# Attention numerators: high and low part of the left operand in one pass

## The chip, the cores and the metric

One core of a Trainium2 chip runs the whole program. The metric is the device time of one execution in microseconds; lower is better. A core has TensorE (PE: matmuls, with its weight loads shown as PEld), VectorE (DVE), ScalarE (ACT), GpSimd (POOL) and SyncE (SP), which issues all the transfers here.

## The reference

The input x has 2048 rows of 1024 columns. It is normalized, goes through a linear attention with 32 heads of 32 columns and through a gated unit, and both are joined:

```
xn = layernorm(x)
q, k, v = split_heads(xn @ wqkv)
phi(a) = concat(softmax(a @ w_phi), softmax(-(a @ w_phi)))   # 64 features a head
kv  = sum over rows of phi(k)^T v          # per head 64 x 32
num = phi(q) @ kv
den = phi(q) . (sum over rows of phi(k)) + 1e-6
s = (num / den) @ wo
g = silu((sigmoid(xn @ w_gate) * (xn @ w_up)) @ w_down)
out = x + s * g
```

All inputs and the output are float32.

## The kernel before

Large products take operands of the type F32R, each float32 operand cut in two parts, with three products in place of one. `split` (L122 to L125) writes a high part with a ScalarE cast (L124) and the rest with a VectorE subtraction (L125). `mm3` (L127 to L131) then adds high x high, high x low and low x high in a bank of PSUM; these are lines 129, 130 and 131 of the profile. The products over blocks use seven block products in place of eight (names B11, T2, T3, B21, T1, T4, B22), which is why there are so many sums of blocks.

The stages follow one another: normalization and the folding of the weights; the projections for the first half of the rows and their gated products; the same for the second half; the down products; the result products. A deque of background tasks is worked off beside the matmuls, one task after certain evacuations. The order of the instructions on each engine is not only that of the source: the program is built with a planner that simulates a timeline (`schedule_with_timeline_sim=True`) and orders what is ready by its own costs. What it writes down for an engine is then fixed.

**Block building.** For each half `hb` of the heads (16 heads), `k_task` and `kv_products` sum phi(k) and v products over all rows. `kv_sum` gathers them, and `kv_blocks` (L471) turns them into left operands: a chunk is 128 rows of features (two heads) and 128 columns, and only the 64 columns of its own two heads are filled. Chunks go in twos, b = 0 and 1: chunk b fills columns 64b to 64b+63, and the other 64 are set to zero. High and low part lie in two planes of a slot. Four chunks make one slot, so a half has two slots; four stores to `kvbd_d` (L489) keep them, and at step n = 20 of the down products four loads (L935) bring them into the slots of `KVB`.

**The attention stage.** There are 8 pairs of row tiles (256 rows). For a pair, `attend` (L672) lists 12 tasks, six for each half of the heads: four `phi_transpose` and two `numerator`, q = 0 and 1 (a quarter of the heads). `phi_transpose` (L625) turns a tile of phi(q), already divided by its denominator, with four transposes (L630) into a bank of the ring `tpr` and splits it. `numerator` (L639) multiplies the four chunks of its quarter with it: chunks 2j and 2j+1 add into the same 256 columns of one bank of the ring `nmr`, which has two banks, so the zeros of one leave the rows of the other alone. A ScalarE copy (L648) takes the whole bank to `oraw[hb]`. After q = 1, `o_operands` (L655) makes the seven blocks from the two halves: splits on ScalarE and VectorE, differences on GpSimd (L660, L663, L664, L668).

The tasks of pair 0 run beside the end of the down products. Those of pair `tp_ + 1` are spread over the 28 `mm3` of the result products of pair `tp_`, whose accumulations use the ring `amm` of four banks. There, B11 is copied to a result buffer by ScalarE (L1008), T2, T3 and the others are added by VectorE (L1010, L1012, L1019, L1022), multiplied and added by GpSimd (L1023, L1024) and stored (L1025). Four result buffers serve a pair and are used again by the next, so the copy at L1008 waits for a store of the pair before.

Of the kernel before, what the change touches and what calls it, by code (L numbers as in the profile page):

```python
# [9 lines left out]
F32 = mybir.dt.float32  # L10
# [7 lines left out]
P = 128  # L18
# [8 lines left out]
HB = 512  # L27
# [21 lines left out]
def hedgehog_glu_kernel(  # L49
# [11 lines left out]
    nc = tc.nc  # L61
# [4 lines left out]
    dram = ctx.enter_context(tc.tile_pool(name="dram", bufs=1, space=DRAM))  # L66
# [8 lines left out]
    e_d = dram.tile([TT, 2, P, 2 * HB], F32, name="e_d")  # L75
    r_d = dram.tile([CTT, 2, P, 32], F32, name="r_d")
    zb_d = dram.tile([2, P, 2 * HB], F32, name="zb_d")
    kvbd_d = dram.tile([4, P, 2, HB], F32, name="kvbd_d")
    ws_d = dram.tile([2 * NJ, 4, P, 2 * HB], F32, name="ws_d")
    h_d = dram.tile([7, NJ, P, NCH, HB], F32, name="h_d")  # L80
    wd_d = dram.tile([7, NJ, P, HB], F32, name="wd_d")
# [3 lines left out]
    slots, blocks, where = {}, {}, {}  # L85

    def block(name, first, n, dtype):
        again = blocks.get(name, (None, 0))[1]
        t = sb.tile([P, n, 2, HB], dtype, name=f"{name}_{again}", tag=name, bufs=1)
        blocks[name] = t, again + 1  # L90
        for i in range(n):
            slots[first + i] = t[:, i]
            where[first + i] = name, i
        return t
# [13 lines left out]
    def whole(i):  # L108
        return slots[i].rearrange("p a n -> p (a n)")
# [9 lines left out]
    def pair(i):  # L119
        return slots[i][:, 0], slots[i][:, 1]  # L120

    def split(o, src):  # L122

        nc.scalar.copy(o[0], src)  # L124
        return nc.vector.tensor_sub(o[1], src, o[0].bitcast(F32))  # L125

    def mm3(o, a, b, first, last, **kw):  # L127

        nc.tensor.matmul(o, a[0], b[0], start=first, stop=False, **kw)  # L129
        nc.tensor.matmul(o, a[0], b[1], start=False, stop=False, **kw)  # L130
        nc.tensor.matmul(o, a[1], b[0], start=False, stop=last, **kw)  # L131

    def cut(ab, s):
        return ab[0][:, s], ab[1][:, s]
# [4 lines left out]
    def step(n=1):  # L139
        for _ in range(min(n, len(side))):  # L140
            side.popleft()()
# [329 lines left out]
    def kv_blocks(hb):  # L471

        s, m = [i.rearrange("p (g f) -> p g f", g=8) for i in (e_k, whole(52))]
        nc.gpsimd.memset(m, 0.0)
        for j in range(4):
            js, fs = slice(j * DH, (j + 1) * DH), slice(j % 2 * 64, j % 2 * 64 + 64)
            nc.scalar.copy(m[js, :, fs], s[js, :, fs])
        for g in range(8):
            nc.tensor.transpose(kvb[g // 4][:, g % 4 * P:(g % 4 + 1) * P], m[:, g], ident)
        for i, o in enumerate((kraw, vraw)):  # L480
            t = slots[53][:, i]
            nc.scalar.copy(t, kvb[i])
            nc.gpsimd.memset(o, 0.0)
            t, o4 = [q.rearrange("p (q b n) -> p q b n", q=2, b=2) for q in (t, o)]
            for b in range(2):
                bs = slice(b * 64, b * 64 + 64)
                nc.vector.tensor_add(o4[:, :, b, bs], t[:, :, b, :64], t[:, :, b, 64:])
            split(pair(36 + i), o)
            nc.sync.dma_start(kvbd_d[2 * hb + i], slots[36 + i].bitcast(F32))  # L489

    ones = sb.tile([P, P], F32R, name="ones")

# [46 lines left out]
    def down_prep():  # L539
        n = len(dready)  # L540
        if n == len(dsteps) or not wfree or len(hfree) < len(dsteps[n][2]):
            return False
        i, j, cs = dsteps[n]
        r = wdraw.next()
        nc.sync.dma_start(r, wd_block(i, j) if i in (B11, B21, B22) else wd_d[i, j])
        w = wfree.popleft()
        split(pair(w), r)
        r = hraw.next()
        hs = {}
        if len(cs) == 2:  # L550
            nc.sync.dma_start(whole(r), h_d[i, j].rearrange("p c n -> p (c n)"))
        for c in cs:
            rc = slots[r][:, c]
            if len(cs) == 1:
                nc.sync.dma_start(rc, h_d[i, j, :, c])
            hs[c] = hfree.popleft()
            last_split[:] = [split(pair(hs[c]), rc).ins]
        dready.append((w, hs))
        return True
# [42 lines left out]


    NTP = TT // 2
    KVB = (36, 37, 38, 43)
    WO = {B11: list(range(8, 12)), T2: list(range(12, 16)), T3: list(range(4, 8)), B21: [],
          T1: [], T4: [], B22: list(range(4))}
    phu = Ring((44, 20))
# [3 lines left out]
    tpr, nmr, amm = Ring(banks[:2]), Ring(banks[2:4]), Ring(banks[4:])  # L612
    e_next, units_ph, of = [0, 0], {}, {}
    oraw = [slots[50], slots[51]]

    def wo_prep(i, k):
        nc.sync.dma_start(slots[WO[i][k]].bitcast(F32), wo_d[i, k])
# [19 lines left out]
            e_load(u)  # L637

    def numerator(tp_, hb, q):  # L639
        ps = nmr.next()  # L640
        ph = units_ph[hb, q]
        kg = [h.rearrange("p (g m) -> p g m", m=P) for h in pair(KVB[2 * hb + q])]
        for j in range(2):
            for b in range(2):
                k = 2 * j + b
                mm3(ps[:, j * 256:(j + 1) * 256], (kg[0][:, k], kg[1][:, k]), (ph[:, 0, k], ph[:, 1, k]), b == 0, b == 1)
        o = oraw[hb].rearrange("p u (g t) -> p u g t", t=P)
        nc.scalar.copy(o[:, :, 2 * q:2 * q + 2], ps.rearrange("p (j u t) -> p u j t", j=2, u=2))  # L648
        if q:
            o_operands(tp_, hb)  # L650

# [3 lines left out]
    def o_operands(tp_, hb):  # L655
        (b11, b12), (b21, b22) = [(o[:, 0], o[:, 1]) for o in oraw]
        if hb == 0:
            of[tp_] = {i: ofr.next() for i in range(7)}
            o_operand(tp_, B11, b11)
            nc.gpsimd.tensor_sub(b11, b12, b11)  # L660
            return
        o_operand(tp_, B22, b22)
        nc.gpsimd.tensor_sub(b12, b22, b12)  # L663
        nc.gpsimd.tensor_sub(b22, b22, b11)  # L664
        o_operand(tp_, T2, b22)
        o_operand(tp_, T3, b12)
        o_operand(tp_, B21, b21)
        nc.gpsimd.tensor_sub(b21, b21, b22)  # L668
        o_operand(tp_, T1, b11)
        o_operand(tp_, T4, b21)  # L670
# [106 lines left out]
    for n, (kind, c, what, i) in enumerate(ops):  # L777
# [23 lines left out]
        j, s = what  # L801
        u = units.index((c, j, s))
# [29 lines left out]
        else:  # L832
            q = {B21: 0, T1: 3, T4: 2, B22: 1}[i]
            g = gates[q]
# [6 lines left out]
            else:  # L841
                if q == 0:
                    nc.vector.tensor_mul(g, g, bank)
                else:
                    b = u1 if q == 1 else u2
# [15 lines left out]
        m = (u % (2 * NJ)) * 7 + glu_order.index(i)  # L861
# [60 lines left out]
    for n, (i, j, cs) in enumerate(dsteps):  # L922
        w, hs = dready[n]
        for c in cs:
            for u in range(4):
                p = 4 * c + u
                mm3(banks[p], cut(pair(hs[c]), slice(u * P, (u + 1) * P)), pair(w),
                    j == 0 and i in (B11, T2, T3, T1), j == NJ - 1, skip_group_check=True)
        wfree.append(w)
        hfree.extend(hs.values())  # L930
        if n >= ND - 2 * NJ - 8 and len(WO[B21]) < 4 and hfree:
            WO[B21].append(hfree.popleft())
        if n == 20:
            for q, s in enumerate(KVB):
                nc.sync.dma_start(slots[s].bitcast(F32), kvbd_d[q])  # L935
        while down_prep():
            pass
        if j == NJ - 1:
            for c in cs:
                for u in range(4):  # L940
                    evacuate(i, 4 * c + u)
        if n and n * 32 // 78 > (n - 1) * 32 // 78 and late:
            t, hb = late.pop(0)
            if t == 0:
                nc.sync.dma_start(zb, zb_d[hb])
            with tc.issue_after(last_split[0]):
                q_task(t, hb)
        if 40 <= n < 56 and n % 2 == 0:
            wo_prep(*divmod((n - 40) // 2, 4))
        if n == ND - 2 * NJ:  # L950
            assert not late and len(WO[B21]) == 4
            block("x1", 4, 4, F32R)
            for i in (T3, B21):
                side.extend([lambda i=i, k=k: wo_prep(i, k) for k in range(4)])
            side.extend([lambda u=u: e_load(u) for u in range(2)])
        if n == ND - NJ:
            step(1000)
            side.extend([lambda fn=fn, a=a: fn(*a) for fn, *a in attend(0)])
        if len(dready) == ND:
            for i, free in ((T1, hfree), (T4, wfree)):  # L960
                while free and len(WO[i]) < 4:
                    WO[i].append(free.popleft())
                    side.append(lambda i=i, k=len(WO[i]) - 1: wo_prep(i, k))
        if n > ND - 2 * NJ:
            step(1 + (n > ND - NJ and n % 2))
# [26 lines left out]
    for tp_ in range(NTP):  # L992
        nxt = attend(tp_ + 1) if tp_ + 1 < NTP else []
        n = 0
        u1, u2, y11, y21 = [res.next() for _ in range(4)]
        for i in range(7):
            if i in opening:
                abank[i] = amm.next()
            ps = abank[{B21: B11, T4: T3, B22: T1}.get(i, i)]
            o = [h.rearrange("p (k t) -> p k t", t=P) for h in pair(of[tp_][i])]  # L1000
# [12 lines left out]
            else:  # L1013
                g, xt = gxs.pop((tp_, i))
                t, cols = rows(tp_, i)
                eng = nc.vector if tp_ == NTP - 1 and i in (T4, B22) else nc.gpsimd
                if i == B21:
                    y = y11
                    nc.vector.tensor_mul(y, g, ps)  # L1019
                else:  # L1020
                    y = {T1: u2, T4: y21, B22: u1}[i]
# [34 lines left out]
```

## Time and profile before

| | |
|---|---|
| median of 3 runs | 2437.62 us (2436.70 to 2439.03) |
| the profiled execution | 2438.41 us, of which 2436.6 us span |
| mean granted TensorE clock | 0.996 |
| busy: PE, PEld, DVE | 2389.2, 1984.5, 1717.3 us |
| busy: ACT, POOL | 1006.8, 989.3 us |
| transfers | 599.44 MB, 246 GB/s mean |
| numerator copies (L648) | first at 2172.4, last at 2411.4 us |
| block building (L477 to L489) | 1241.8 to 1590.3 us |

The span is from the first to the last instruction; the rest of the time lies around it. Lines of the profile name the source line, the engine, the operation, output and inputs by the program's tile names (fa, fb, fc, x, w, p are blocks of slots), shapes and counts. Matmuls overlap, so the duration of one (0.28 us for 256 columns) is longer than the step to the next. "Idle" behind a group is what its engine stood still just before it, with what ended that.

### The profile page before, as it was taken

Reading aid. Unit: us, or ns where it says so; the run is one execution under the profiler, and the core shown is the slowest. Engines: PE = TensorE matmul, PEld = TensorE weight load, DVE = VectorE, ACT = ScalarE, POOL = GpSimd, SP = SyncE. Lnnn points to the kernel's source line nnn. Section 1 sums busy time; section 2 is a strip of 40 time slices with the busy share of each in tenths; the row PEclk is TensorE's granted clock in tenths of the full one; section 3 lists DMA queues with packets and bytes.
Section 4 is the critical chain, followed back from the end, with each engine's and each line's share of the span. In section 5 each row is a group of like instructions: output and inputs, shape, how many; then the busy total and the mean of one; then the engine's idle time right before and its main releaser. Section 6 shows DMA issues by size and latency. Waiting matters only on the chain.

```text
span 2436.6 us, 32010 instructions
## 1 busy us (share of the span) xinstructions
PE 2389.2 (98%) x11076; PEld 1984.5 (81%) x11076; DVE 1717.3 (70%) x2247; ACT 1006.8 (41%) x1499; POOL 989.3 (41%) x665
## 2 busy tenths in 40 slices
PE   7999999999999999999999999999999999999998
PEld 6788778888888878888888888888888888888887
DVE  6535577778777679747867888646888988855454
ACT  6432344444444344314444444423443334453332
POOL 5540255756656442222353222323333335414554
PEclk8999999999999999999999999999999999999999
DMA  7887787767777787777777666587666666867554
GB/s 275 271 300 248 255 299 259 271 248 268 260 261 249 255 293 249 265 263 250 261 267 272 221 215 224 191 288 247 221 233 238 217 209 229 286 233 251 173 178 147
DMA packets 233234, 599.44 MB, mean 246 GB/s; under 512 B 30576, under 2 KB 30576, under 8 KB 228464
## 3 DMA queue, kind: packets, MB, share of 16 engines
q1 hardware_dynamic: 233072, 597.40, 71.8%
q8 instruction: 87, 1.43, 0.2%
q14 instruction: 75, 0.61, 0.1%
HBM read 361.10 MB, written 236.19 MB: 245 GB/s over the span
## 4 chain that ended last, share of the span: by engine, by line
PE 74%; DMA 7%; DVE 7%; issue 5%; POOL 4%; ACT 2%; SPq 0%; ACTq 0%; POOLq 0%; DVEq 0%
PE bank L129 24%; PE bank L131 24%; PE bank L130 24%; DMA wo_d<-fc 3%; DVE w L125 1%; PE bank L458 1%; DVE x L125 1%; PE bank L630 1%; DVE p L125 1%; DMA fb<-wqkT 1%; DMA fc<-xo_d 1%; PE bank L278 0%; DVE fc L125 0%; DMA out<-fc 0%; DMA fc<-wo 0%
## 5 line engine op out<-in xcount | busy, mean ns | idle before, releaser
L129 PE MATMUL bank<-x,w 128*128 128x512 f32 x2352 | 912.8, 390 | 8.0 <-ACT fb L837 2.3
L130 PE MATMUL bank<-x,w 128*128 128x512 f32 x2352 | 915.7, 389 | 0.0
L131 PE MATMUL bank<-x,w 128*128 128x512 f32 x2352 | 907.1, 389 | 0.0
L129 PEld LDWEIGHTS bank<-x,w 128*128 128x128 f32 x2352 | 441.5, 188 | 102.9 <-ACT fb L837 2.7
L131 PEld LDWEIGHTS bank<-x,w 128*128 128x128 f32 x2352 | 441.6, 188 | 92.0 <-DVE w L125 0.4
L124 ACT CAST w<-fa 128x512 fp32r<-128x512 f32 (+1 forms) x444 | 307.6, 697 | 504.7 <-PE bank L130 371.0
L130 PEld LDWEIGHTS bank<-x,w 128*128 128x128 f32 x2352 | 441.7, 188 | 90.2 <-DVE x L125 0.3
L125 DVE TENSOR_TENSOR w<-fa,w 128x512 fp32r<-128x512 f32 (+1 forms) x444 | 438.5, 992 | 108.7 <-ACT w L124 101.6
L129 PE MATMUL bank<-w,x 128*128 128x512 f32 x708 | 279.5, 395 | 7.8 <-DVE fc L388 3.2
L131 PE MATMUL bank<-w,x 128*128 128x512 f32 x708 | 277.8, 393 | 1.8 <-DVE x L125 1.8
L130 PE MATMUL bank<-w,x 128*128 128x512 f32 x708 | 277.3, 392 | 0.0
L847 POOL TENSOR_TENSOR fb<-fb,fc 128x512 f32<-128x512 f32 x57 | 88.9, 1560 | 243.3 <-DVE fc L846 218.2
L129 PEld LDWEIGHTS bank<-w,x 128*128 128x128 f32 x708 | 133.8, 189 | 38.9 <-DVE fc L388 3.4
L131 PEld LDWEIGHTS bank<-w,x 128*128 128x128 f32 x708 | 133.5, 189 | 29.8 <-DVE x L125 2.5
L130 PEld LDWEIGHTS bank<-w,x 128*128 128x128 f32 x708 | 133.9, 189 | 26.8
L587 POOL TENSOR_TENSOR fc<-fc 128x1024 f32<-128x1024 f32 x32 | 81.5, 2548 | 182.0 <-ACT fc L423 127.5
L846 DVE TENSOR_TENSOR fc<-fc,bank 128x512 f32<-128x512 f32 x84 | 57.4, 684 | 103.7 <-PE bank L131 92.8
L125 DVE TENSOR_TENSOR x<-fa,x 128x512 fp32r<-128x512 f32 x112 | 114.7, 1024 | 18.0 <-ACT x L124 17.9
L125 DVE TENSOR_TENSOR w<-fb,w 128x512 fp32r<-128x512 f32 (+1 forms) x114 | 102.4, 899 | 32.8 <-ACT w L124 31.1
L124 ACT CAST w<-fb 128x512 fp32r<-128x512 f32 (+1 forms) x114 | 71.3, 626 | 118.7 <-PE bank L130 97.0
L599 POOL TENSOR_TENSOR fc<-fc,sa 128x1024 f32<-128x1024 f32 x32 | 70.4, 2199 | 101.1 <-DVE sa L596 101.1
L847 POOL TENSOR_TENSOR fc<-fc 128x512 f32<-128x512 f32 x27 | 43.4, 1608 | 134.8 <-DVE fc L846 106.9
(246 smaller groups left out, 3281.1 us busy)
## 6 DMA issues: line engine op xcount, KB each, us to landing
ws_d<-w SPq DMA_DIRECT2D x112, 512.0 KB, 4.2
w<-ws_d SPq DMA_DIRECT2D x112, 512.0 KB, 5.0
fa<-w_gu SPq DMA_DIRECT2D x84, 512.0 KB, 4.2
fa<-h_d SPq DMA_DIRECT2D x84, 512.0 KB, 4.3
fa<-wf_d SPq DMA_DIRECT2D x32, 1024.0 KB, 6.3
h_d<-fc SPq DMA_DIRECT2D x120, 256.0 KB, 3.6
fc<-e_d SPq DMA_DIRECT2D x48, 512.0 KB, 3.7
fc<-qkv_d SPq DMA_DIRECT2D x80, 256.0 KB, 4.7
```

The costliest lines, as they stand in the source:

```text
L124: nc.scalar.copy(o[0], src)
L125: return nc.vector.tensor_sub(o[1], src, o[0].bitcast(F32))
L129: nc.tensor.matmul(o, a[0], b[0], start=first, stop=False, **kw)
L130: nc.tensor.matmul(o, a[0], b[1], start=False, stop=False, **kw)
L131: nc.tensor.matmul(o, a[1], b[0], start=False, stop=last, **kw)
L458: nc.tensor.matmul(kvb[g // 2][:, g % 2 * 256:g % 2 * 256 + 256], v[:, g].rearrange("p a f -> p (a f)"), ph[:, g].rearrange("p a f -> p (a ...
L587: nc.gpsimd.tensor_mul(ez, e, zb)
L599: nc.gpsimd.tensor_mul(e3, e3, r2[:, :, None].to_broadcast([P, 32, DH]))
L630: nc.tensor.transpose(ps[:, j * P:(j + 1) * P], e[:, k * P:(k + 1) * P], ident)
L846: v = nc.vector.tensor_add(b, u2 if q == 3 else u1, bank)
L847: nc.gpsimd.tensor_mul(g, g, b)
```

## The change

The zero columns of a chunk now hold its low part. The left operand of chunk b has the high part in columns 64b to 64b+63 and the low part in the other 64. One matmul with the high part of phi(q) and one with its low part then give four part products: the rows of the chunk's own half of the bank hold those with the high part, the other rows those with the low part. The two chunks of a pair cannot add into one bank any more, so chunks b = 0 go to one bank and chunks b = 1 to the other. For each, a ScalarE copy takes the 64 rows of the low shares to the 64 rows of the output, and a VectorE add puts the 64 rows of the high shares on top. A half needs one slot in place of two, so stores and loads of the blocks are halved, and the memsets go.

```diff
-    kvbd_d = dram.tile([4, P, 2, HB], F32, name="kvbd_d")
+    kvbd_d = dram.tile([2, P, 2 * HB], F32, name="kvbd_d")
...
             nc.scalar.copy(t, kvb[i])
-            nc.gpsimd.memset(o, 0.0)
-            t, o4 = [q.rearrange("p (q b n) -> p q b n", q=2, b=2) for q in (t, o)]
+            t, o = [q.rearrange("p (q b n) -> p q b n", q=2, b=2) for q in (t, o)]
+            nc.vector.tensor_add(o[:, :, :, :64], t[:, :, :, :64], t[:, :, :, 64:])
+
+            k = slots[36][:, i].rearrange("p (q b a n) -> p q b a n", q=2, b=2, a=2)
             for b in range(2):
-                bs = slice(b * 64, b * 64 + 64)
-                nc.vector.tensor_add(o4[:, :, b, bs], t[:, :, b, :64], t[:, :, b, 64:])
-            split(pair(36 + i), o)
-            nc.sync.dma_start(kvbd_d[2 * hb + i], slots[36 + i].bitcast(F32))
+                split((k[:, :, b, b], k[:, :, b, 1 - b]), o[:, :, b, :64])
+        nc.sync.dma_start(kvbd_d[hb], slots[36].bitcast(F32).rearrange("p a n -> p (a n)"))
...
-    KVB = (36, 37, 38, 43)
+    KVB = (36, 37)
...
     def numerator(tp_, hb, q):
-        ps = nmr.next()
         ph = units_ph[hb, q]
-        kg = [h.rearrange("p (g m) -> p g m", m=P) for h in pair(KVB[2 * hb + q])]
-        for j in range(2):
-            for b in range(2):
+        kg = slots[KVB[hb]][:, q].rearrange("p (k m) -> p k m", m=P)
+        for b in range(2):
+            ps = nmr.next()
+            for j in range(2):
                 k = 2 * j + b
-                mm3(ps[:, j * 256:(j + 1) * 256], (kg[0][:, k], kg[1][:, k]), (ph[:, 0, k], ph[:, 1, k]), b == 0, b == 1)
-        o = oraw[hb].rearrange("p u (g t) -> p u g t", t=P)
-        nc.scalar.copy(o[:, :, 2 * q:2 * q + 2], ps.rearrange("p (j u t) -> p u j t", j=2, u=2))
+                for a in range(2):
+                    nc.tensor.matmul(ps[:, j * 256:(j + 1) * 256], kg[:, k], ph[:, a, k], start=a == 0, stop=a == 1)
+            hi, lo = [slice(r * 64, r * 64 + 64) for r in (b, 1 - b)]
+            o = oraw[hb][hi].rearrange("p u (g t) -> p g u t", t=P)[:, 2 * q:2 * q + 2]
+            y, z = [ps[r].rearrange("p (j u t) -> p j u t", j=2, u=2) for r in (hi, lo)]
+            nc.scalar.copy(o, z)
+            nc.vector.tensor_add(o, o, y)
         if q:
             o_operands(tp_, hb)
...
         if n == 20:
-            for q, s in enumerate(KVB):
-                nc.sync.dma_start(slots[s].bitcast(F32), kvbd_d[q])
+            for hb, s in enumerate(KVB):
+                nc.sync.dma_start(slots[s].bitcast(F32).rearrange("p a n -> p (a n)"), kvbd_d[hb])
```

## The prediction

> **What bounds the kernel now.** I read the page first. The first two lines below are from its first part (busy time, share, instructions), the third from its slices. Then I read the windows view of the stretch in which the edited products run, and the waits of TensorE from there to the end.
>
> ```profile
> PE 2389.2 (98%) x11076; PEld 1984.5 (81%) x11076; DVE 1717.3 (70%) x2247; ACT 1006.8 (41%) x1499; POOL 989.3 (41%) x665
> ...
> PEclk8999999999999999999999999999999999999999
> ...
> 2172.00:2411.00 239.00, 234.90 (x1318) 201.35 (x1319) 124.19 (x171) 92.02 (x166) 114.03 (x82) 1.00 0.59 195
> ...
> PE bank L129 <- DVE fc L1012: 1.6, 1, 1.6
> PE bank L630 <- DVE x L125: 1.4, 3, 0.5
> PE bank L129 <- ACT fa L124: 1.4, 1, 1.4
> PE bank L129 <- ACT fc L1008: 1.4, 1, 1.4
> ```
>
> TensorE is the bound, at full granted clock. Between 2172 and 2411 us it is busy 234.9 of 239.0 us, VectorE 124.2 (52%), ScalarE 92.0 (38%), GpSimd 114.0. A matmul taken off its queue there is time, unless an operand or a bank comes late in its place. Busy matmuls overlap, so the price of one is its start-to-start step. The timeline of TensorE gives it:
>
> ```profile
> 2307.05 0.28 PE L129 MATMUL bank<-x,p 128*128 128x256 f32 x1
> 2307.16 0.28 PE L130 MATMUL bank<-x,p 128*128 128x256 f32 x1
> 2307.28 0.28 PE L131 MATMUL bank<-x,p 128*128 128x256 f32 x1
> ...
> 2308.36 0.28 PE L131 MATMUL bank<-x,p 128*128 128x256 f32 x1
> 2308.48 0.40 PE L131 MATMUL bank<-x,x 128*128 128x512 f32 x1
> ```
>
> Those are one numerator call: 12 matmuls from 2307.05 to 2308.48, 0.119 us each, though one lasts 0.28.
>
> **The change part by part.** *Products removed.* There are 8 pairs of row tiles, 2 halves of the heads, 2 quarters each: 32 calls. Each falls from 12 matmuls (4 chunks, 3 products) to 8 (4 chunks, 2 products) of the same 128x256 shape: 128 fewer, 128 x 0.119 = 15.2 us. That the two new products of a chunk share their left operand gains nothing further: L129 and L130 already share theirs, and L130 has as many weight loads as matmuls.
>
> The Trainium skill, "TensorE: Matmul & The Clock Gate", section Back-to-back issue gap, gives a sustained 81 ns per load-and-matmul pair at 128 columns and 131 ns at 512; on a line between them 256 columns would be an estimated 98 ns, the saving 12.5 us and my sum below 2.7 us poorer. This trace disagrees (119 ns at 256 columns, 227 to 231 at 512), so the trace's step is used.
>
> *Evacuation added.* Each call had one ScalarE copy of 128x512 out of the bank. Now it has two copies and two VectorE adds of 64 rows. The nearest rows:
>
> ```profile
> L648 ACT COPY fc<-bank x32: 586/587/589, 2172.4 to 2411.4; 128x512 f32<-128x512 f32 x32
> ...
> L1022 DVE TENSOR_TENSOR fc<-fc,bank 128x512 f32<-128x512 f32 x21 | 14.4, 685 | 20.1 <-PE bank L131 20.0
> ...
> L477 ACT COPY fc<-fc x8: 616/618/622, 1241.8 to 1570.4; 32x512 f32<-32x512 f32 x8
> ```
>
> The 32-row copy of L477 takes 0.618 us, as long as the casts of 128 rows from SBUF (0.626), so I give 64 rows the full price: a copy 0.587, an add 0.685. No row shows a 64-row add; its ends are half of 0.685 (if rows counted) and the 0.97 of SBUF-to-SBUF subtractions that run beside GpSimd. I take 0.685, same operands and length. ScalarE gains 32 x 0.587 = 18.8 us and VectorE 64 x 0.685 = 43.8 us, over 239 us: 46% and 70%. Neither becomes the bound; by volume this costs nothing. If that cover went, its whole price would be the 43.8 us.
>
> *Longer chain behind a call.* Before, from the last matmul to data in SBUF: 0.03 us hand-over (matmul ends 2323.30, copy starts 2323.33) and 0.59. After, counted from the end of the first bank's matmuls: copy done at 0.62, add at 1.34; second copy done at 1.21, second add, behind the first, at 2.03. The last matmul ends at 0.48 (4 x 0.119), so the chain is 1.55 instead of 0.62: 0.9 us longer. The splits and differences (o_operands) for the next pair wait for this, queued behind it on VectorE and GpSimd. Where is that felt? At three of the pairs' boundaries TensorE already waits for the low part of a split; one is
>
> ```profile
> 2327.34 0.40 PE L130 MATMUL bank<-x,fa 128*128 128x512 f32 x1
> 2328.20 0.66 PE L630 MATMUL bank<-ident,fc 128*128 128x128 f32 x4 [0.47 <-DVE x L125]
> 2329.28 0.50 PE L131 MATMUL bank<-x,fa 128*128 128x512 f32 x1 [0.42 <-DVE fa L125]
> ```
>
> The other two come about 60 us before and after. There the 0.9 is charged in full: 3 x 0.9 = 2.7 us. At the others the operands are ready and I charge nothing. Ends: 0 (the order shifts and hides it) and 8 x 0.9 = 7.2 us.
>
> *A chain that does not shrink.* At every second boundary the copy of B11 (L1008) waits for a result buffer: products of B22, evacuation, two GpSimd steps, store. In the timelines TensorE waits 1.36 us for it at 2298.41, 1.37 at 2415.68 (a cast queued behind L1008), and just meets it near 2356 with about 0.4 to spare. A half's two calls lie inside that chain, so their saving, 8 x 0.119 = 0.95 us, only lengthens the wait: 0.95 + 0.95 + 0.55 = 2.45 us lost again. Ends: 0 and 4 x 0.95 = 3.8.
>
> *Banks.* The two banks used to alternate between calls; now one call takes both. After a call the first bank is free 1.37 us after its last matmul there, and a call right behind wants it after 0.48: 0.9 us. In the before order between 3 and 6 matmuls of 512 columns (0.7 to 1.4 us) stand around such a pair, and the planner can put more there: I take 0. The other end is the first rival.
>
> *Block building (kv_blocks) and its transfers.* Off: 4 memsets (0.53 us each, L483), 4 of 8 VectorE adds (0.82 mean, L487), 2 of 4 stores and 2 of 4 loads of 512 KB, 0.32 us of SP's queue each. The 2 splits per half become 4 of a quarter of the width (4 instructions to 8). All of it runs between 1241 and 1667 us, where TensorE is busy 299.65 of 300 and 300 of 300 and no wait names these lines; between +1 and -1 us, taken as 0. The cover is the projections' and GLU's matmuls; without it the shorter work would be a gain of a few us. On SP nothing moves past another wait; the loads (L935) only get fewer.
>
> Sum: -15.2 + 2.7 + 2.45 = -10.1 us. The profiled execution took 2438.4 us (span 2436.6 and 1.8 around it) and would take 2428.3; the median of the runs is 2437.6, 0.8 below it, so the forecast is 2427.5.
>
> **The rivals.** *Evacuation holds TensorE (slower).* 16 second calls of a half follow a first call closely. If nothing else stands ready, each waits 0.9 us for the first bank and 0.2 for the second, and the add may stand behind one split on VectorE (0.69): 16 x 1.8 = 28.6 us, with the charges above +18.5, so 2456. It turns slower once such a pair loses more than 10.1/16 = 0.63 us. For it: runs of VectorE without a gap, 2324.4 to 2332.1. Against it: VectorE is idle for nearly half of the stage, and 84 matmuls of the result products per pair give work to put in between. Chance 0.15. The Trainium skill, "TensorEngine Tiling (Array Packing)", section PSUM Bottleneck, says that making TensorE's part quicker does not speed up the emptying of PSUM, which can then be the limit; this trace has evacuation far from that, at 52% and 38% busy.
>
> *The chains set the pace.* The period of two pairs is 58.5 us (numerator copies at 2308.68 and 2367.17). If operand chain and result buffers, not TensorE, hold it there, only the pair prepared inside the down products keeps its saving, 16 x 0.119 = 1.9 us: 2435.7. Against it: two pairs need by steps 168 x 0.230 + 96 x 0.119 + 16 x 0.45 (a group of four transposes) = 57.3 us of TensorE, so it is 98% full. Chance 0.12, spread over -5 to +1.
>
> *All of it arrives.* The planner hides both boundary losses: -15.2, 2422.4. Chance 0.23.
>
> *It does not save.* If the load of the left operand (0.19 us) set the step, or sharing it hurt, 256 matmuls at 0.18 would take as long as 384 at 0.119: no change. The steps of 0.119 beside loads of 0.19 speak against it. Chance 0.03.
>
> **How the numbers follow.** The forecast, -10 with its own range of -5 to -13, has 0.47. About 0.2%, 4.9 us, is what a measurement of this kernel can tell from no change. Faster: the forecast, the full saving and some of the pace rival: 0.75. Same: most of that rival, the last one and the mild edge of the first: 0.12. Slower: the first rival's rest: 0.13. The order of all engines after the block building is planned anew; from the 5 to 10 us that TensorE idles after 2172 I allow 2 us either way. Low end: the full saving and 2 more, 2420. High end: the edge of the first rival, 2439; beyond lie its 0.13 and a little at the bottom.
>
> **What would show it.** Right: 128 fewer matmuls and loads; numerators still at 0.119; two copies and two adds per call at 0.59 and 0.69; the period of two pairs near 56 us instead of 58.5 (3.8 less, some 1.3 given back); waits of TensorE grown by about 5 us, behind L125 and L1008. Wrong: 64-row adds much dearer than 0.69; waits of numerators for their own bank's add or copy; a period that stays at 58.5; a stage before 1241 us that moves.

## The result and the profile after

The change makes the kernel slower: 2449.83 us median (2442.01 to 2454.93) against 2437.37 for the kernel before, ratio 1.0052, 95% interval 1.004 to 1.0064, some 12.7 us. The forecast was 2427.5. The profiled execution took 2453.17 us (span 2451.4), mean granted clock 0.991; that of before took 2438.41 and had 0.996. In the lines of after the source has moved: the numerators' matmuls are L648, their copies L652, their adds L653, the copy of B11 is L1013, the store of a result L1030.

The first part of the page and its row of the granted clock, after:

```profile
PE 2388.1 (97%) x10948; PEld 1978.2 (81%) x10948; DVE 1755.4 (72%) x2311; ACT 1026.8 (42%) x1535; POOL 991.3 (40%) x661
PEclk8999999999999999999999999999999999999998
```

There are 128 matmuls and 128 loads fewer, as the change says, 64 more instructions on VectorE, and TensorE's busy time fell by only 1.1 us. The clock is the first sign of why. The windows view from the first copy of B11 to the last, of before and then of after (length, then busy time of PE, PEld, DVE, ACT, POOL, granted clock, DMA share, GB/s):

```profile
2206.98:2414.00 207.02, 203.01 (x1152) 174.19 (x1150) 101.76 (x140) 74.70 (x134) 106.92 (x77) 1.00 0.59 192
```

```profile
2209.85:2423.80 213.95, 198.11 (x1035) 165.36 (x1034) 135.62 (x194) 91.73 (x162) 108.56 (x76) 0.97 0.56 184
```

Seven pairs lie in it, with 7 x 16 = 112 matmuls fewer, 112 x 0.119 = 13.3 us less work. The stretch is 6.9 us longer all the same: two pairs take 61.1 us (213.95 / 3.5) instead of 59.1, where the prediction looked for 56. TensorE stands idle 213.95 - 198.11 = 15.8 us instead of 4.0, 11.8 more, and its busy time fell by 4.9 instead of 13.3. These 8.4 us went for the most part into matmuls at a lower clock; more on that below. Behind the last copy of B11 the span has 27.6 us instead of 22.6, 5.0 more. The first copy comes 2.9 us later; after was already 3.6 us behind at about 1220 us, ahead of anything that the change reorders, so this is scatter from one execution to another. 6.9 + 5.0 + 2.9 = 14.8, the difference of the two spans.

The largest of TensorE's waits from 2165 us to the end, after (line and what it waited for: us in all, times, longest):

```profile
PE bank L630 <- DVE x L125: 10.5, 5, 2.9
PE bank L129 <- ACT fa L124: 5.5, 1, 5.5
PE bank L129 <- DVE fc L1017: 3.2, 7, 1.4
```

The transposes' bank waits for a split, 10.5 us in place of 1.4. No matmul of a numerator waits for a copy or an add of its own bank. The split is late because of ScalarE. Its waits for a store, in the same view of before and of after:

```profile
ACT fc L1008 <- DMA out<-fc: 4.8, 3, 2.4
```

```profile
ACT fc L1013 <- DMA out<-fc: 28.5, 6, 6.6
```

It is the wait that the prediction priced at 2.45 us. ScalarE's timeline of after shows what it blocks (start, duration, operation; in brackets the idle time ahead and its end):

```profile
2292.49 0.59 ACT L124 CAST fb<-bank 128x512 fp32r<-128x512 f32 x1 [0.34 <-PE bank L630]
2297.74 0.59 ACT L1013 COPY fc<-bank 128x512 f32<-128x512 f32 x1 [4.66 <-DMA out<-fc]
2298.35 0.58 ACT L652 COPY fc<-bank 64x512 f32<-64x512 f32 x1
2298.95 0.58 ACT L124 CAST x<-bank 128x512 fp32r<-128x512 f32 x1
2299.56 0.58 ACT L652 COPY fc<-bank 64x512 f32<-64x512 f32 x1
2300.16 0.59 ACT L124 CAST fb<-bank 128x512 fp32r<-128x512 f32 x1
```

The store was issued by SP at 2294.58 and landed at 2297.74. Until then ScalarE did nothing, with two numerator copies and two casts queued behind L1013 that needed no store. The casts are the high parts of the transposed rows: their low parts (L125) follow on VectorE, and TensorE's next transposes need the bank that these free. TensorE starts again at 2300.32, after 1.87 us. Not all of the 4.66 us is lost, since the first copy queued behind L1013 has to wait for its numerators anyway. Their matmuls are

```profile
2296.43 1.11 PE L648 MATMUL bank<-x,p 128*128 128x256 f32 x8
```

and in the run rot_after below the same copy starts 0.67 us after the first of them. Here that would be about 2297.10, an estimate; it started at 2298.35, so the store put it off by some 1.25 us.

In the planned order of after the copy of B11 stands ahead of two numerator copies in nearly every pair, and six of its eight executions wait for a store. Before it stood ahead of them in every second pair, and its three waits fall in the other pairs, where the numerator copies are already done. The order was planned anew with the new instructions; why the planner chose it is not known.

Behind some of these waits TensorE ran at a lower clock. Its timeline of after:

```profile
2393.04 1.12 PE L630 MATMUL bank<-ident,fc 128*128 128x128 f32 x4 [2.91 <-DVE x L125]
...
2427.65 0.80 PE L129 MATMUL bank<-w,fa 128*128 128x512 f32 x1 [5.55 <-ACT fa L124]
2428.24 0.63 PE L130 MATMUL bank<-w,fa 128*128 128x512 f32 x1
2428.67 0.63 PE L129 MATMUL bank<-x,fa 128*128 128x512 f32 x1
2429.09 0.63 PE L130 MATMUL bank<-x,fa 128*128 128x512 f32 x1
```

The steps are 0.43 us here instead of 0.23. The windows of the four stretches at a lower clock, after:

```profile
2269.64:2273.05 3.41, 3.27 (x14) 2.92 (x14) 3.38 (x6) 2.20 (x5) 2.60 (x2) 0.50 0.48 154
2331.08:2334.49 3.41, 3.27 (x16) 2.93 (x15) 3.38 (x6) 2.23 (x5) 2.31 (x2) 0.50 0.49 154
2392.52:2399.35 6.83, 6.31 (x23) 5.54 (x23) 6.77 (x9) 5.33 (x10) 4.48 (x3) 0.50 0.26 80
2426.65:2433.48 6.83, 5.83 (x14) 4.45 (x15) 5.74 (x5) 2.81 (x5) 4.32 (x3) 0.50 0.00 0
```

The first three lie between the first and the last copy of B11. TensorE was busy for 3.27 + 3.27 + 6.31 = 12.9 us in them; at half the clock about 6.4 us of that is lost, an estimate. The other 2.0 of the 8.4 us no view explains.

The waits ahead of these stretches are 2.09 us (ending at 2269.01), 1.98 (2330.74), 2.91 and 5.55 us; waits of 1.87 us (2300.32) and 1.67 us (2361.71) had no lower clock behind them. The length of one wait does not decide it. In other runs a wait of 1.73 us was followed by a clock of 0.50 (evac_only, 2233.25), and waits of 2.44 us (phi3, 2276.17) and 3.21 us (rot_no_add, 2151.45) were not. The Trainium skill, "TensorE: Matmul & The Clock Gate", section What's actually happening, puts the fall to half rate behind an idle window of about 3.4 us that runs freely. The half rate agrees (0.50), and the stretches of 3.4 and 6.8 us are one and two such windows. The length of the idle time does not agree as it stands: less than 2.0 us of listed idle time were enough here, and the measurement decides.

### The profile page after: what moved, and what is told of

It reads as the page before. It is cut to its first block, busy times and chain, and to the rows that moved or that the text cites. A ratio compares the mean times of both kernels' runs of the same rounds, so it can differ in the third digit from the quotient of the medians.

```text
span 2451.4 us, 31875 instructions
## 1 busy us (share of the span) xinstructions
PE 2388.1 (97%) x10948; PEld 1978.2 (81%) x10948; DVE 1755.4 (72%) x2311; ACT 1026.8 (42%) x1535; POOL 991.3 (40%) x661
## 4 chain that ended last, share of the span: by engine, by line
PE 74%; DVE 7%; DMA 7%; issue 6%; POOL 4%; ACT 2%; SPq 0%; ACTq 0%; POOLq 0%; DVEq 0%
PE bank L129 24%; PE bank L130 24%; PE bank L131 24%; DMA wo_d<-fc 2%; DVE w L125 1%; DVE x L125 1%; PE bank L458 1%; POOL fc L1029 1%; DMA fc<-xo_d 1%; POOL fc L1028 1%; DMA out<-fc 1%; DVE p L125 1%; ACT x L124 0%; PE bank L630 0%; PE bank L648 0%
## 5 line engine op out<-in xcount | busy, mean ns | idle before, releaser
L125 DVE TENSOR_TENSOR w<-fa,w 128x512 fp32r<-128x512 f32 (+1 forms) x444 | 436.8, 988 | 101.7 <-ACT w L124 95.6
L851 DVE TENSOR_TENSOR fc<-fc,bank 128x512 f32<-128x512 f32 x84 | 57.3, 683 | 102.5 <-PE bank L131 91.8
L125 DVE TENSOR_TENSOR x<-fa,x 128x512 fp32r<-128x512 f32 x112 | 112.0, 1000 | 20.8 <-ACT x L124 20.5
L125 DVE TENSOR_TENSOR w<-fb,w 128x512 fp32r<-128x512 f32 (+1 forms) x114 | 102.4, 899 | 33.0 <-ACT w L124 31.4
```

The source lines that it names most:

```text
L851: v = nc.vector.tensor_add(b, u2 if q == 3 else u1, bank)
```

## The experiments

All comparisons are against the kernel before on the same chip. The table sums up; "us" is (ratio - 1) x 2438, "store" is ScalarE's waits for a store, and "PE" the sum of the rows of TensorE's waits, both from 2165 us on in the profiled execution.

| kernel | median | ratio, 95% interval | us | store | PE |
|---|---|---|---|---|---|
| before | 2437.4 | 1 | 0 | 4.8 | 7.7 |
| after | 2449.83 | 1.0052 [1.004, 1.0064] | +12.7 | 28.5 | 22.0 |
| rot_after | 2435.39 | 0.9989 [0.998, 0.9997] | -2.7 | none | 11.6 |
| rot_before | 2434.18 | 0.9977 [0.9968, 0.9986] | -5.6 | none | 3.3 |
| prod_only | 2425.87 | 0.9944 [0.9931, 0.9958] | -13.7 | 10.8 | 8.5 |
| evac_only | 2455.75 | 1.0072 [1.0058, 1.0086] | +17.6 | 19.0 | 19.2 |
| rot_prod | 2423.97 | 0.9936 [0.9919, 0.9952] | -15.6 | none | 5.7 |
| rot_no_add | 2429.92 | 0.9952 [0.9933, 0.9971] | -11.7 | none | 8.5 |
| rot_one_bank | 2432.27 | 0.9967 [0.9952, 0.9982] | -8.0 | none | 8.2 |
| rot_tr_first | 2433.99 | 0.9978 [0.9967, 0.9988] | -5.4 | none | 12.3 |
| e_ahead | 2422.79 | 0.9936 [0.992, 0.9953] | -15.6 | none | 4.6 |
| phi3 | 2434.90 | 0.998 [0.997, 0.9989] | -4.9 | none | 14.4 |
| tr_first_before | 2432.04 | 0.997 [0.9957, 0.9982] | -7.3 | none | 2.7 |
| e_only | 2433.39 | 0.9984 [0.9976, 0.9993] | -3.9 | none | 10.9 |
| e_ahead_prod | 2418.35 | 0.9924 [0.9911, 0.9936] | -18.5 | none | 3.4 |
| e_ahead_store | 2433.29 | 0.998 [0.9968, 0.9992] | -4.9 | 17.0 | 11.4 |

Theory A: the copy of B11, waiting for its store at the head of ScalarE's queue, takes the saving and more. Its rival B: copying and adding two banks is dear by itself, and the store only came last.

**rot_after: the change without the wait for the store.** The result buffers are handed on so that B11's copy gets one that was stored early.

```diff
+    u1, u2, y11, y21 = [res.next() for _ in range(4)]
     for tp_ in range(NTP):
-        u1, u2, y11, y21 = [res.next() for _ in range(4)]
+        if tp_:
+            u1, u2, y11, y21 = y11, u2, y21, u1
```

> The changed kernel with the four result buffers handed round: the copy of B11 takes the buffer that the pair before stored first, not last. The planned order of the instructions is nearly the same on every engine (ScalarE's the same). Theory A (in the changed kernel ScalarE's queue is held at that copy by a store of the pair before, and the numerator copies and casts planned behind it hold TensorE, whose clock then drops too): the waits of about 2 us per pair go, two pairs take 53 to 56 us in place of 61.5, and the time is 2422 to 2430, below the kernel before. Theory B (two banks per call, emptied by a copy and an add, are what holds TensorE): the period stays at 60 or more and the time at 2445 to 2455.

2435.39 us, 0.9989: 15.4 us less than the change by the two ratios, some 3.6 us either way. In the traces the orders of the two programs are the same but for 1 of 1535 instructions on ScalarE (a copy of B11 that comes earlier in the second pair), 13 of 10948 on TensorE, 3 of 2311 on VectorE and 1 of 661 on GpSimd, so this is the wait and what hangs on it: TensorE's waits fall from 22.0 to 11.6 us, and the time at a clock of 0.50 within the stage from some 20 us to 3.4. ScalarE, and then TensorE, at the same place:

```profile
2290.80 0.59 ACT L1015 COPY fc<-bank 128x512 f32<-128x512 f32 x1 [0.81 <-PE bank L131]
2294.03 0.58 ACT L652 COPY fc<-bank 64x512 f32<-64x512 f32 x1 [2.65 <-PE bank L648]
...
2293.36 1.11 PE L648 MATMUL bank<-x,p 128*128 128x256 f32 x8
2296.00 0.66 PE L630 MATMUL bank<-ident,fc 128*128 128x128 f32 x4 [0.63 <-DVE x L125]
```

The copy goes as soon as B11 is there, and the next waits for its numerators. TensorE's wait is 0.63 us instead of 1.87. Theory B does not hold. Theory A named the cause, but its range (2422 to 2430) is missed: it expected that the whole saving would then appear, and some 12 us of it are still missing.

**rot_before: the same on the kernel before.**

> The kernel before with the same hand-round of result buffers. Theory A: its copies of B11 wait for a store at every second pair, 1.4 us twice on TensorE: 2433 to 2437. Theory B says nothing of it: 2437.

2434.18 us, -5.6, in theory A's range. The wait was worth far less there than in the change: ScalarE waited 4.8 us for stores instead of 28.5, and TensorE's waits fall from 7.7 to 3.3. With buffers handed on in both, the change is still 2.9 us the slower one (rot_after against rot_before), though the intervals overlap.

**prod_only and evac_only: the change's two halves alone.** The first has the 8 products in one bank and one copy of 128 rows; the second has the 12 products of before, with two banks, two copies and two adds.

```diff
 prod_only, against the change
-        for b in range(2):
-            ps = nmr.next()
-            for j in range(2):
+        ps = nmr.next()
+        for j in range(2):
+            for b in range(2):
...
-            nc.scalar.copy(o, z)
-            nc.vector.tensor_add(o, o, y)
+        nc.scalar.copy(o[:, :, 2 * q:2 * q + 2], ps.rearrange("p (j u t) -> p u j t", j=2, u=2))
```

```diff
 evac_only, against before
-        ps = nmr.next()
...
+        for b in range(2):
+            ps = nmr.next()
+            for j in range(2):
                 k = 2 * j + b
...
+            nc.scalar.copy(o, z)
+            nc.vector.tensor_add(o, o, y)
```

> Only the products of the change: 8 matmuls per call into one bank, one copy of 128 rows as before. It leaves out that the high and low shares are kept apart and added. Theory A and B both: the saving of TensorE is real without the added evacuation, 2422 to 2430. If 256 matmuls of shared operands cost as much as 384 (theory C), 2435 to 2440.

> Only the evacuation of the change: the 12 products of before, with the zeros, chunks b = 0 and 1 in two banks, two copies and two adds per call. Theory A: dear only through what stands behind the copy of B11 in ScalarE's plan, which has it ahead of numerator copies in every second pair: 2440 to 2452. Theory B: the two banks themselves cost 1 us or more a call, and with longer products more: 2460 or more.

The products alone gain 13.7 us (10.2 to 16.8), which holds the 15.2 of the prediction. The evacuation alone costs 17.6 us, between the two theories' ranges. It brings the wait for the store with it, though no product has changed:

```profile
ACT fc L1011 <- DMA out<-fc: 19.0, 7, 4.6
```

So the added copies and adds seem to call up both: an order with the wait at the head, and something of their own. The two halves do not add up: -13.7 + 17.6 = 3.9 us, and the whole change costs 12.7. Each edit is planned anew as a whole. One more thing shows in prod_only: it waits 10.8 us for stores and keeps its gain. Such a wait costs only where what is queued behind it is needed soon.

**rot_prod, rot_no_add, rot_one_bank: what the rest consists of.** The first is prod_only with the buffers handed on, the second rot_after without the adds (`nc.scalar.copy(o, y)` alone), the third rot_after with all products in one bank and still two copies and two adds, which mixes the sums of the two chunks. Theory D: the adds on VectorE; theory E: the second bank.

> The products of the change into one bank with one copy (high and low shares not kept apart, as in prod_only), and the result buffers handed round. What TensorE can reach in this stage: two pairs in 53.6 to 55 us, 2419 to 2424. Against rot_after (2435) it gives the whole price of the added evacuation without the wait for a store, some 12 to 15 us.

> rot_after without the adds and with the copies taking the high shares: two banks, two copies of 64 rows, the low shares left out. Theory D (the rest of the loss is VectorE's 64 adds, which stand in its queue ahead of the splits of phi that TensorE waits for): close to rot_prod, 2420 to 2426. Theory E (one call taking both banks is the rest): close to rot_after, 2432 to 2436.

> rot_after with both chunks of a call added into one bank (shares not kept apart), but the two copies and two adds kept. Theory D: near rot_after, 2431 to 2438. Theory E: near rot_prod, 2420 to 2426.

Between rot_after and rot_prod lie 12.9 us. Without the adds 9.0 of them go, with one bank 5.3; the intervals of these differences are some 4 to 5 us either way. Neither theory has it all. VectorE's timeline of rot_after shows D's mechanism:

```profile
2294.64 0.68 DVE L653 TENSOR_TENSOR fc<-fc,bank 64x512 f32<-64x512 f32 x1 [3.63 <-ACT fc L652]
2295.26 0.69 DVE L125 TENSOR_TENSOR x<-bank,x 128x512 fp32r<-128x512 f32 x1
2295.98 0.69 DVE L653 TENSOR_TENSOR fc<-fc,bank 64x512 f32<-64x512 f32 x1
2296.70 0.69 DVE L125 TENSOR_TENSOR fb<-bank,fb 128x512 fp32r<-128x512 f32 x1
```

An add stands ahead of each low part (L125), and TensorE waits for these: 0.63 us at 2296.00 and 0.34 at 2297.45, and much the same in three or four other pairs.

**rot_tr_first: the transposes ahead of the calls.** If the splits stand behind adds, all four transposes of a half should come first.

```diff
-            out += [tr[0, 0], tr[0, 1], tr[1, 0], nm[0], tr[1, 1], nm[1]]
+            out += [tr[0, 0], tr[1, 0], tr[0, 1], tr[1, 1], nm[0], nm[1]]
```

> rot_after with the four transposes of a half listed ahead of its two numerator calls, so that the casts and subtractions of phi come before the copies and adds in both queues where the planner keeps the order. Theory D: the waits of TensorE for a split of phi (0.63 and 0.34 us per pair) go, 2424 to 2432. Theory E: calls that follow each other closer wait more for their banks, 2435 or more.

2433.99 us, between the two ranges, and 2.7 us below rot_after with overlapping intervals: little. A new wait has come; the largest of TensorE's waits of rot_tr_first:

```profile
PE bank L630 <- DMA fc<-e_d: 4.4, 3, 3.6
PE bank L630 <- DVE fb L125: 2.6, 4, 1.6
PE bank L129 <- ACT fa L124: 2.1, 1, 2.1
```

The rows to be transposed are loaded into two slots that the transposes of the half before free. The earlier these are wanted, the more the loads show.

**e_ahead, phi3, tr_first_before: where that leads.** The change leaves two slots free (38 and 43). In e_ahead they take the rows of e, one half further ahead; in phi3 they make a third buffer for the transposed rows; tr_first_before is a control, the kernel before with buffers handed on and the new order.

```diff
 e_ahead, against rot_tr_first
+    EB = ((47, 48), (38, 43))
...
-            nc.sync.dma_start(whole(47 + u), e_d[2 * tp_ + u, hb])
+            nc.sync.dma_start(whole(EB[hb][u]).bitcast(F32), e_d[2 * tp_ + u, hb])
...
-            side.extend([lambda u=u: e_load(u) for u in range(2)])
+            side.extend([lambda u=u: e_load(u % 2) for u in range(4)])
```

> rot_tr_first (result buffers handed round, all four transposes of a half ahead of its two calls) with the e rows of a half loaded one half further ahead, into the two slots that the change leaves free. In rot_tr_first TensorE waited 4.4 us in all, three times, at L630 for loads of e_d. Theory F: those waits are path; without them the time falls by about 3 to 5 us, to 2429 to 2431. Theory G: the evacuation by ScalarE and VectorE sets the pace there, and the load only came last: 2433 to 2436, with the waits now behind a DVE or ACT row.

> rot_tr_first with a third buffer for the transposed rows (the blocks move to the two free slots, their old two become the buffer). Theory F (the loads of e_d hold the transposes back): no change, 2432 to 2436, and the waits at L630 for e_d stay. Theory H: with two buffers the transposes of the next half wait until the calls have read them, and through them the loads: 2428 to 2431.

> A control: the kernel before with the result buffers handed round (2434.2 when it was timed) and all four transposes of a half ahead of its two calls. There are no adds of halves on VectorE here. If the order only helps by taking the second transposes out from behind those adds, it does nothing or costs a little here: 2433 to 2437. If it is better by itself: 2429 to 2432, and what rot_tr_first gained is not to be put down to the adds.

e_ahead takes 2422.79 us, 15.6 less than before, with both banks, both copies and both adds in place. The loads were the path, as theory F says, but it expected 3 to 5 us and 10.2 came (rot_tr_first to e_ahead). Theory H (the third buffer) does not hold. TensorE's waits of e_ahead:

```profile
PE bank L129 <- ACT fa L124: 2.1, 1, 2.1
PE bank L129 <- DVE fc L1020: 1.4, 1, 1.4
PE bank L131 <- DVE x L125: 0.5, 1, 0.5
PE bank L649 <- ACT fb L124: 0.4, 1, 0.4
PE bank L631 <- DVE fb L125: 0.2, 1, 0.2
```

Copies of B11 stand 26.6 us apart in the mean (2207.13 to 2393.23, seven pairs). By the prediction's steps two pairs needed 57.3 us of TensorE before, now 57.3 - 32 x 0.119 = 53.5, or 26.7 a pair. TensorE is the bound again. That e_ahead's 15.6 is so near the 15.2 of the forecast is chance, because the handing on and the order of tasks help the kernel before too: the control gains 7.3, so that 8.3 us are left for the change and its early loads. Between the first and the last copy of B11 the two compare like this, the control first:

```profile
2206.48:2405.34 198.86, 198.35 (x1130) 170.85 (x1129) 105.45 (x140) 75.22 (x134) 104.67 (x76) 1.00 0.59 195
...
2207.13:2393.23 186.10, 185.13 (x1024) 158.17 (x1023) 140.69 (x194) 91.21 (x162) 105.00 (x76) 1.00 0.59 200
```

TensorE has hardly any idle time in either, and the stretch is 12.8 us shorter, of the 13.3 that 112 matmuls make. So the saving does arrive there. Behind the last copy e_ahead takes 3.5 us longer (28.2 against 24.7), with a wait of 2.1 us and a clock of 0.50 for 3.4 us.

By its ratio the control lies in the range of "better by itself" (2438 - 7.3 = 2430.7), but its gain is within the interval of rot_before's 5.6, so that the order by itself does something without the adds is not shown.

**e_only, e_ahead_prod, e_ahead_store: which part of e_ahead does it.** e_only has the early loads but the change's order of tasks; e_ahead_prod is e_ahead with prod_only's evacuation; e_ahead_store is e_ahead without the handing on.

> rot_after (result buffers handed round) with the e rows loaded one half further ahead into the two free slots, and the order of transposes and calls as the change has it. Theory F (the rows of e come late, and the transposes are bunched behind them): most of what e_ahead gained comes from this alone, 2421 to 2427. Theory I (it takes both, since the second transposes stand behind the adds on VectorE as well): 2428 to 2434. Theory G (the adds and banks have a price of 11 to 12 us whatever the loads do): 2433 to 2437.

> e_ahead with the evacuation of prod_only in place of the change's: both products' chunks into one bank and one copy of 128 rows, no adds (the shares of the two halves of rows are not kept apart). Theory F: with the rows of e loaded ahead the copies and adds are hidden, so this is as fast as e_ahead: 2420 to 2425. Theory G: the evacuation still costs a part, and taking it away gives 4 us or more: 2412 to 2419.

> e_ahead with the result buffers in the order that the change has (not handed round), so that the copy of B11 waits again for the store of the pair before. Theory A (that wait, at the head of ScalarE's queue, is a cost of its own): 8 to 15 us above e_ahead, 2431 to 2438. If it only hurt because the transposes had no time to spare: within 3 us of e_ahead, 2421 to 2426.

e_only, 2433.39, gains next to nothing on rot_after: its waits for the splits are those of rot_after. It takes both, the order and the loads; each alone shows the other's wait. e_ahead_prod has its median in theory G's range, 4.4 us below e_ahead; by the ratios it is 2.9 below, and the intervals overlap: of the 12.9 us that adds and bank had seemed to cost, some 3 are left, and none is not excluded. e_ahead_store is 10.7 us above e_ahead, and the store is back:

```profile
ACT fc L1014 <- DMA out<-fc: 17.0, 7, 4.2
```

Its order was planned anew, so the 10.7 are not the wait alone; but theory A's size, 8 to 15, holds. TensorE's largest wait in it is one that after does not have: numerators waiting for an add to empty their own bank (PE bank L649 <- DVE fc L654, 2.7 us in two waits). e_ahead beats both kernels and every other version that keeps the shares of the two halves of rows apart.

## Why the prediction was wrong

**What held.** *Products removed* (15.2): 128 fewer, prod_only gained 13.7, and e_ahead needs 12.8 of 13.3 us less than its control between the copies of B11. The step of the new products stayed 0.119 us. *Block building* at nothing: no wait names it, and the 3.6 us at about 1220 us stand ahead of it. The prices of 64 rows held; the lines view of after:

```profile
L652 ACT COPY fc<-bank x64: 577/581/587, 2177.0 to 2425.0; 64x512 f32<-64x512 f32 x64
...
L653 DVE TENSOR_TENSOR fc<-fc,bank x64: 669/686/692, 2177.7 to 2425.7; 64x512 f32<-64x512 f32 x64
```

**The step that failed: *A chain that does not shrink*, and with it the 2 us for the new plan.** It had the right place, the store ahead of B11's copy, but took it for a chain with the wait in every second pair, as in the order of before, and asked only by how much it would grow: 2.45 us, at most 3.8. In the new order the copy stands at the head of ScalarE's queue in nearly every pair, 28.5 us of waits instead of 4.8, ahead of copies and casts that TensorE's transposes need. Measured: 15.4 us (after against rot_after), part of it the lower clock behind the longer waits. The new plan had been allowed 2 us either way; that is the term that was too small. The prediction itself named the wait and the cast queued behind it, and did not ask what a different order would put there.

**The clock.** The sum had no term for it. Of the 20.2 us lost between the first and last copy of B11 (13.3 saved, 6.9 longer), 11.8 are idle time, and of the other 8.4 about 6.4 are the lower clock.

**The second step that failed: *Longer chain* 2.7, *Banks* 0, volume 0.** Together they came to 12.9 us (rot_after against rot_prod) in the planned order; without the adds 9.0 of them go, with one bank 5.3. The prediction charged the longer chain only at three pairs' boundaries. The runs show waits in most pairs: an add stands ahead of a split in VectorE's queue, and once that order is changed, the rows of e come late. By volume it was right that neither engine becomes the bound: between the copies of B11 VectorE was busy 63% and ScalarE 43% of the time (forecast 70% and 46%). With the transposes and loads moved ahead 2.9 are left; that this is near the 2.7 is luck, in another order than the one priced. The runs make a chain: -15.6 (rot_prod) + 12.9 + 15.4 = +12.7, where the sum had -15.2 + 2.7 + 2.45.

**The rivals.** *Evacuation holds TensorE*, 2456, has the right sign and a nearer size than the forecast, by another way: in after no numerator waited for its own bank. Of its clause of an add behind a split on VectorE the reverse is seen, the split behind the add. *The chains set the pace* describes rot_after better than the forecast does: its pairs take 28.1 us each (2209.88 to 2406.48) though TensorE needs 26.7, and the chain is e rows, transposes, splits behind adds. Its 2435.7 is close to rot_after's time by chance, since it was meant for the change itself.

**Still open.** Why the planner chose that order from two copies more is not known. How the 12.9 us divide between adds and bank is known to some 4 to 5 us. Why the early loads gave 10.2 us, when the waits that they took away were 4.4, is open as well.

## What to carry to other kernels

When an edit adds instructions to an engine whose order is planned, look at every instruction of that engine's queue that waits for something slow, a store above all, and price what it would block if it came to stand one place earlier; a margin for "the new order" should be of that size. Take such a wait away (here by handing buffers on) before judging the edit. Buffers that a change frees may be worth nearly as much as its saved work: here the early loads gave 10.2 us, once the buffers were handed on and the transposes came first. Give the kernel before the same help when the worth of the change is asked for: of the 15.6 us that e_ahead gained, the control without the change had 7.3.

## What was unexpected of the hardware

Behind some waits of TensorE its granted clock was 0.50 for 3.4 or 6.8 us, with steps of 0.43 us instead of 0.23 for 512 columns. A wait of 1.73 us had that behind it (evac_only), and one of 3.21 us had not (rot_no_add), so the length of a wait alone does not tell. A 64-row copy or add out of a bank takes as long as one of 128 rows (0.581 and 0.686 us against 0.587 and 0.685).
